# A scan-and-feed-forward kernel: early small reads of the weights, and the masks of two pairs issued in twos

## The chip, the cores and the metric

The kernel runs on one core of one Trainium2 chip. The metric is the device time of one execution in microseconds. Engines are named as in the profile: PE multiplies matrices (PEld loads its weights), DVE is the vector engine, ACT the scalar engine, POOL is GpSimd, SP is the engine that mostly issues DMAs.

## The reference

Two layers follow each other. The first is a chunked state-space scan with 4 batches, 8 heads, 768 positions, 32 channels a head and 16 states; the second is a feed-forward layer with a squared ReLU. Cut to what is computed:

```python
# per batch and head, chunks of 32 positions
cum  = np.cumsum(log_a[chunk]); L = np.exp(cum[i] - cum[j]) * (i >= j)
y    = ((C @ B.T) * L) @ x + (C @ state) * np.exp(cum)
state = np.exp(cum[-1]) * state + sum_j(B[j] x[j] * np.exp(cum[-1] - cum[j]))
# then, over the 3072 tokens, heads side by side (256 features)
h   = np.maximum(y @ w_in, 0.0)      # w_in  256 x 2048
out = h * h @ w_out                  # w_out 2048 x 256
```

The inputs are float32; the two weights are 2 MB each.

## The kernel before

The 3072 tokens are 12 *pairs* (k = 0 to 11), each a batch b and a stretch j of 256 positions; pair k is also block k of the feed-forward layer. A chunk in the kernel is not 32 positions: each pair is treated as two halves of 128 (u = 0, 1), with even and odd positions apart (r = 0, 1). "Third pair" in the change's name is k = 2, "fourth pair" k = 3.

For a pair, the loads of C, B and x come from `ph_load` (line 121; SP issues them), with a hardware queue for SP and another for ACT. The decays come from `a` once for all pairs: `a_nat`, clipped to `a_cl`, scanned to `cp_r`, spread by PE with the matrix `sel` made from the constants `cf` (lines 446, 447, 492 to 530). From there a pair takes these steps:

- `prep_c`, `prep_b`, `prep_x` (lines 145 to 176): scaled copies of C, B and x in bf16, for later pairs on POOL. `prep_x` gives `xs`.
- `ph_tr`, and for k from 4 on a DMA transpose (`ph_dtr`): B and C with states on the partitions, `bct` (line 210).
- `ph_mt` (line 220): PE forms the products of C and B in two PSUM tiles, `mt`, which hold two groups q each.
- `ph_mask` (line 231): DVE multiplies each of the four groups q = 0 to 3 by the causal mask in `cb`, from PSUM to SBUF: `mts`.
- `ph_u` (line 249): PE's update of the state from B and `xs`; `ph_s` (lines 272 to 293) makes the states.
- `ph_y` (lines 307 to 340): the outputs Y from `mts`, `xs` and the states; ACT copies them to `T` (line 359), the feed-forward layer's input.

The feed-forward layer of a block is 8 *steps*, each 256 of the 2048 features: `mm1` (line 370, PE into one of two PSUM slots `hps`), ReLU by ACT to `hb` (line 376), `square` by DVE to `h` (line 382), and `mm2` (line 400) into `ops`. Its weights sit in SBUF as bf16. POOL issues their loads, with a conversion from float32: `load_wi` (line 129) in eight parts of 256 columns of every w_in row, `load_wo` (line 134) in four parts of 512 rows of w_out. They are issued as the work needs them: w_in's first four parts at 4.8 to 9.8 us, w_out's first two from 9.8 us.

The order of all work is written by hand. `steps` lists 96 steps (block, part); for each step s the loop at the end of the kernel issues `mm1`, then what `todo` holds for s (filled by `at`), then the square of step s-1, then an `mm2`, which lags 3 steps, and 4 from step 17 on. So within DVE's queue a mask placed at step s stands ahead of the square of step s-1. Blocks 0 and 1 share the first 16 steps; from step 16 the blocks come one by one. `first_steps` gives the steps of pairs 2 and 3: transposes, U, states, mt, the four masks in a tuple, and Y. Each engine works through its own queue in order, and waits on semaphores. Eight semaphores serve the hardware-queue DMAs in rotation: a DMA waits for the one eight before it.

Of the kernel before, what the change touches and what calls it, by code (L numbers as in the profile page):

```python
# [10 lines left out]
FP32 = mybir.dt.float32  # L11
# [5 lines left out]
def _fap(base: bass.AP, offset_elems: int, free_dims):  # L17

    ap0 = list(base.ap)[0]
    return bass.AP(tensor=base.tensor, offset=base.offset + offset_elems,  # L20
                   ap=[list(ap0)] + [list(d) for d in free_dims])


def _dap(base: bass.AP, offset_elems: int, dims):

    return bass.AP(tensor=base.tensor, offset=base.offset + offset_elems,
                   ap=[list(d) for d in dims])
# [3 lines left out]
def kernel(  # L31
# [14 lines left out]
    nc = tc.nc  # L46
# [5 lines left out]
    const = ctx.enter_context(tc.tile_pool(name="const", bufs=1))  # L52
# [60 lines left out]
    def ph_load(k, order="CBx", eng=None, gate=None):  # L113
        b, j = PAIRS[k]
        t = loaded.setdefault(k, {})
        for what in order:
            src, w = {"B": (B, N), "C": (C, N), "x": (x, D)}[what]
            dst = nat.tile([128, NH, 2 * w], FP32, tag=f"{what}_nat", name=f"{what}_nat{k}")
            if gate is not None:
                gate.memset(dst[:, 0, 0:1], 0.0)  # L120
            (eng or nc.sync).dma_start(
                out=dst, in_=_dap(src, (b * NH * S + j * 256) * w,
                                  [[2 * w, 128], [S * w, NH], [1, 2 * w]]))
            t[what] = dst
# [320 lines left out]
    with tc.manual_schedule():  # L445
        nc.sync.dma_start(out=a_nat, in_=_dap(a, 0, [[256, 96], [1, 256]]))
        nc.scalar.dma_start(out=cf, in_=cf_d.ap())
        ph_load(0, "C")
        ph_load(0, "B")

# [52 lines left out]
        for r in range(2):  # L503
            nc.scalar.copy(out=_fap(C_r, r * 128, [[16, 2], [32, 4], [1, 16]]),
                           in_=_fap(loaded[0]["C"], r * 16, [[128, 2], [32, 4], [1, 16]]))
# [66 lines left out]
        def at(s, fn, *args):  # L572
            todo.setdefault(max(s, 0), []).append((fn, args))
# [18 lines left out]
        for j, s in ((1, 13), (2, 45)):  # L592
            at(s, recip, 0, 4, j)
        first_steps = {
            2: (9, 12, 12, 10, (10, 11, 11, 12), 14),
            3: (17, 21, 21, 18, (18, 19, 19, 20), 22)}
        at(0, ph_mt, 1)
        at(0, warm, 1, 256)
        for i in (1, 0):
# [87 lines left out]
```

## Time and profile before

| | |
|---|---|
| median of 8 runs | 118.78 us |
| lowest and highest | 116.92 and 121.58 us |
| the profiled execution | 117.82 us |
| its span | 116.1 us |
| outside the span | 1.7 us |
| mean DMA rate over the span | 116 GB/s |
| packets under 512 B | 44352 of 50963 |

The profile is of one execution. "Busy" is the time in which an engine works on an instruction; the slices cut the span in 40 parts of 2.9 us. A wait line names the engine and line that waited, after the arrow what released it, then the sum in us, how often, and the longest. A timeline line gives the start, the time from start to end of a group of like instructions, and how many they are; for PE, groups overlap a little since matmuls are pipelined. SPq and ACTq are the issues of DMAs on SP and ACT.

### The profile page before, as it was taken

The numbers are of one execution on the slowest core, as the hardware profiler recorded it, in microseconds if no ns is written. First come the engines' busy times: TensorE is split into PE (matmuls) and PEld (weight loads), VectorE is DVE, ScalarE is ACT, GpSimd is POOL, SyncE is SP. The second block draws the span as 40 slices with busy tenths as digits, with TensorE's granted clock in tenths as the row PEclk, the third lists the DMA queues.
The fourth block names the chain that finished last, engine by engine and source line by source line (L and its number), as shares of the span: only waits on it lengthen the run. The fifth ranks groups of instructions, "written<-read, shape, count | busy, mean of one in ns | idle before, by whom it ended". The sixth has DMA issues, their size and how long they took to land.

```text
span 116.1 us, 4011 instructions
## 1 busy us (share of the span) xinstructions
PE 109.1 (94%) x1639; PEld 88.4 (76%) x1639; DVE 87.0 (75%) x205; ACT 76.1 (66%) x145; POOL 39.0 (34%) x80
## 2 busy tenths in 40 slices
PE   5989879999999999999999999999999999999980
PEld 2545568777787788788887887887887887888970
DVE  6689937599699799798896984994966966935440
ACT  5465957757867577586677586675775865966830
POOL 4669949048594440350414602604300000000000
PEclk9999999999999999999999999999999999999999
DMA  3999999999799812866918628539050020020202
GB/s 71 204 143 151 124 197 180 182 168 177 143 245 228 152 28 90 159 125 126 183 53 162 130 74 160 111 117 217 19 161 3 0 96 0 20 76 0 90 6 90
DMA packets 50963, 13.53 MB, mean 116 GB/s; under 512 B 44352, under 2 KB 50048, under 8 KB 50944
## 3 DMA queue, kind: packets, MB, share of 16 engines
q1 hardware_dynamic: 46400, 10.98, 45.0%
q0 software_dynamic: 4288, 2.10, 14.4%
q8 instruction: 13, 0.21, 0.8%
q10 hardware_dynamic: 256, 0.18, 0.6%
q14 instruction: 6, 0.05, 0.2%
HBM read 10.64 MB, written 3.15 MB: 119 GB/s over the span
## 4 chain that ended last, share of the span: by engine, by line
PE 73%; DMA 14%; DVE 5%; POOL 3%; issue 1%; ACT 0%; SPq 0%; DVEq 0%; POOLq 0%
PE ops L400 31%; PE hps L370 29%; DMA x_nat<-in_x_dram 8%; DMA w_in_b<-in_moe_w_in_dram 4%; PE Y L307 3%; PE mt L220 3%; DMA C_nat<-in_C_dram 2%; DVE mts L231 2%; POOL xs L176 2%; PE Y L336 2%; DVE h L382 1%; PE U L249 1%; PE ctpt L509 1%; PE ops_r L400 1%; DVE bct L526 1%; PE ops L416 1%
## 5 line engine op out<-in xcount | busy, mean ns | idle before, releaser
L376 ACT ACTIVATE hb<-hps 128x512 bf16<-128x512 f32 x96 | 57.5, 599 | 29.7 <-PE hps L370 28.0
L370 PE MATMUL hps<-T,w_in_b 128*128 128x256 bf16 x384 | 57.6, 273 | 0.5 <-DMA w_in_b<-in_moe_w_in_dram 0.3
L400 PE MATMUL ops<-w_out_b,h 128*128 128x256 bf16 x360 | 55.0, 273 | 0.6 <-DMA w_out_b<-in_moe_w_out_dram 0.6
L382 DVE TENSOR_TENSOR h<-hb 128x512 bf16<-128x512 bf16 x96 | 41.6, 457 | 11.1 <-ACT hb L376 11.0
L370 PEld LDWEIGHTS <-w_in_b 128*128 128x128 bf16 x384 | 37.2, 98 | 5.1 <-DMA w_in_b<-in_moe_w_in_dram 0.5
L400 PEld LDWEIGHTS <-h 128*128 128x128 bf16 x376 | 34.5, 98 | 7.0 <-issue 2.6
L231 DVE TENSOR_TENSOR mts<-mt,cb 128x512 bf16<-128x512 f32 x44 | 29.1, 683 | 8.6 <-PE mt L220 8.5
L176 POOL TENSOR_TENSOR xs<-x_nat,Pinv 128x512 bf16<-128x512 f32 x12 | 13.8, 1154 | 10.4 <-DMA x_nat<-in_x_dram 4.0
L145 POOL TENSOR_TENSOR bc<-C_nat,P_sb 128x128 bf16<-128x128 f32 x16 | 6.7, 440 | 24.7 <-DMA C_nat<-in_C_dram 24.7
L293 DVE TENSOR_TENSOR S<-z,Pown 128x256 bf16<-128x256 f32 x16 | 7.9, 496 | 0.5
L485 PE MATMUL dps<-dum 128*128 128x256 bf16 (+1 forms) x25 | 6.3, 366 | 1.3 <-DVE dum L451 1.3
L359 ACT CAST T<-Y 128x512 bf16<-128x512 f32 x11 | 6.4, 586 | 1.1 <-PE Y L340 1.1
L438 ACT COPY osb<-ops 128x512 f32<-128x512 f32 x11 | 6.4, 580 | 0.0
L129 POOL DMA_DIRECT2D w_in_b<-in_moe_w_in_dram x8 | 6.0, 752 | 0.0
L220 PE MATMUL mt<-bct 32*64 32x256 bf16 x192 | 5.1, 280 | 0.3 <-DVE bct L210 0.2
L307 PE MATMUL Y<-mts,xs 64*32 64x128 bf16 x384 | 5.1, 219 | 0.2 <-DVE mts L231 0.2
L170 POOL CAST bc<-B_nat 128x128 bf16<-128x128 f32 x16 | 4.6, 318 | 2.0 <-DMA B_nat<-in_B_dram 1.7
L485 PEld LDWEIGHTS <-dum 128*128 128x128 bf16 x25 | 2.4, 112 | 3.3 <-issue 1.8
L307 PEld LDWEIGHTS <-xs 64*32 64x32 bf16 x384 | 3.1, 91 | 1.9 <-issue 1.0
L220 PEld LDWEIGHTS <-bct 32*64 32x64 bf16 x192 | 1.9, 102 | 2.9 <-issue 1.7
L286 DVE SCALAR_TENSOR_TENSOR z<-z,Ptot,U 128x64 f32<-128x64 f32 x12 | 3.2, 266 | 0.5 <-PE U L249 0.5
L134 POOL DMA_DIRECT2D w_out_b<-in_moe_w_out_dram x4 | 3.1, 792 | 0.3 <-issue 0.3
(77 smaller groups left out, 57.2 us busy)
## 6 DMA issues: line engine op xcount, KB each, us to landing
x_nat<-in_x_dram SPq DMA_DIRECT2D x12, 256.0 KB, 3.7
out_dram<-osb SPq DMA_DIRECT2D x7, 256.0 KB, 2.7
C_nat<-in_C_dram SPq DMA_DIRECT2D x12, 128.0 KB, 2.9
B_nat<-in_B_dram SPq DMA_DIRECT2D x12, 128.0 KB, 3.3
w_in_b<-in_moe_w_in_dram POOLq DMA_DIRECT2D x8, 128.0 KB, 5.6
w_out_b<-in_moe_w_out_dram POOLq DMA_DIRECT2D x4, 256.0 KB, 6.5
out_dram<-osb SPq DMA_DIRECT2D x8, 128.0 KB, 2.3
bct<-bc SPq DMA_TRANSPOSE x8, 3.4
```

The costliest lines, as they stand in the source:

```text
L145: eng.tensor_tensor(out=_fap(bc[k % 3], r * 384 + 128, [[144, 2], [32, 4], [1, 16]]), in0=_fap(loaded[k]["C"], r * 16, [[128, 2], [32, 4], ...
L176: eng.tensor_tensor(out=_fap(xs, 0, [[256, 2], [32, 8], [1, 32]]), in0=_fap(loaded[k]["x"], 0, [[32, 2], [64, 8], [1, 32]]), in1=_fap(Pinv ...
L220: nc.tensor.matmul(mt[q // 2][64 * u:64 * u + 64, q % 2, r, :, :], bct[32 * q:32 * q + 32, r, 0, u * 64:u * 64 + 64], _fap(bct[32 * q:32 * ...
L231: nc.vector.tensor_tensor(out=v["mts"][:, q], in0=v["mt"][q // 2][:, q % 2] if src is None else src, in1=_fap(cb, 128, [[128, 2], [0, 2], ...
L293: nc.vector.tensor_tensor(out=S_n.rearrange("p (g q d) -> p g q d", g=2, q=4), in0=_fap(z, 0, [[32, 2], [0, 4], [1, 32]]), in1=_fap(Pown, ...
L307: nc.tensor.matmul(Y[u][32 * q:32 * q + 32, g, :], v["xs"][64 * u:64 * u + 64, r, h * 32:h * 32 + 32], v["mts"][64 * u:64 * u + 64, q, r, ...
L359: nc.scalar.copy(out=_fap(T[k], 0, [[64, 2], [128, 4], [1, 64]]), in_=_fap(Y[0], 0, [[512, 2], [64, 4], [1, 64]]))
L370: nc.tensor.matmul(hps[:, i, :], w_in_b[:, g, f * 128:(f + 1) * 128], T[blk][:, g].rearrange("p r u t -> p (r u t)"), start=(g == 0), stop ...
L376: nc.scalar.activation(out=hb, in_=hps, func=AF.Relu)
L382: nc.vector.tensor_tensor(out=h2, in0=hb, in1=hb, op=ALU.mult)
L400: nc.tensor.matmul(o[c], h2[:, i, r * 128:(r + 1) * 128], w_out_b[:, f, c * 128:(c + 1) * 128] if len(o) > 1 else w_out_b[:, f, :], start= ...
L485: nc.tensor.matmul(idle[-1][:, 0:cols], dum[:, 0:128], dum[:, 0:cols], start=True, stop=True, skip_group_check=True)
```

## The change

A tile `ahead` is added, which nothing reads. Right after the load of `cf`, ACT issues two more loads: 64 bytes from the start of each of the 256 rows of w_in (8 KB apart), and 64 bytes from every 16 KB of w_out (128 places). In program order they stand after the loads of `a` and `cf`, and before the first loads of C and B.

The masks of pair 2 go from steps (10, 11, 11, 12) to (10, 10, 11, 11), and those of pair 3 from (18, 19, 19, 20) to (18, 18, 19, 19). On DVE the order mask 0, square, masks 1 and 2, square, mask 3, square becomes masks 0 and 1, square, masks 2 and 3, square, square. Nothing else moves on PE, POOL or SP; two more DMAs in the rotation make two of SP's early loads wait for a semaphore.

```diff
         nc.sync.dma_start(out=a_nat, in_=_dap(a, 0, [[256, 96], [1, 256]]))
         nc.scalar.dma_start(out=cf, in_=cf_d.ap())
+
+        ahead = const.tile([128, 3, 16], FP32, name="ahead")
+        nc.scalar.dma_start(out=ahead[:, 0:2, :], in_=_dap(moe_w_in, 0, [[2048, 128], [128 * 2048, 2], [1, 16]]))
+        nc.scalar.dma_start(out=ahead[:, 2, :], in_=_dap(moe_w_out, 0, [[4096, 128], [1, 16]]))
         ph_load(0, "C")
         ph_load(0, "B")
...
         first_steps = {
-            2: (9, 12, 12, 10, (10, 11, 11, 12), 14),
-            3: (17, 21, 21, 18, (18, 19, 19, 20), 22)}
+            2: (9, 12, 12, 10, (10, 10, 11, 11), 14),
+            3: (17, 21, 21, 18, (18, 18, 19, 19), 22)}
```

## The prediction

> **What bounds the kernel now.** I read the page first: engine shares and slices. PE is busy for 94% of the span, at full clock throughout, and its idle tenths stand in the first slices and the last.
>
> ```profile
> PE 109.1 (94%) x1639; PEld 88.4 (76%) x1639; DVE 87.0 (75%) x205; ACT 76.1 (66%) x145; POOL 39.0 (34%) x80
> PE   5989879999999999999999999999999999999980
> DMA  3999999999799812866918628539050020020202
> ```
>
> The rest is therefore read between 0 and 40 us, where the 16 DMA engines are full too. Next the list of PE's waits. Small as they are, they are all that this change can reach:
>
> ```profile
> PE ops L400 <- DMA w_out_b<-in_moe_w_out_dram: 0.6, 1, 0.6
> PE hps L370 <- DMA w_in_b<-in_moe_w_in_dram: 0.3, 1, 0.3
> PE mt L220 <- DVE bct L210: 0.2, 1, 0.2
> PE U L249 <- POOL xs L176: 0.2, 1, 0.2
> PE Y L307 <- DVE mts L231: 0.2, 1, 0.2
> ```
>
> The timeline places them. Columns: start, duration, engine, line, work, count, and idle time before with its releaser.
>
> ```profile
> 13.92 0.61 PE L370 MATMUL hps<-T,w_in_b 128*128 128x256 bf16 x4 [0.33 <-DMA w_in_b<-in_moe_w_in_dram]
> 15.68 0.60 PE L400 MATMUL ops<-w_out_b,h 128*128 128x256 bf16 x4 [0.59 <-DMA w_out_b<-in_moe_w_out_dram]
> ...
> 23.52 1.33 POOL L176 TENSOR_TENSOR xs<-x_nat,Pinv 128x512 bf16<-128x512 f32 x1 [3.08 <-DMA x_nat<-in_x_dram]
> 24.91 0.25 PE L249 MATMUL U<-xs,Bb 64*32 64x64 bf16 x16 [0.20 <-POOL xs L176]
> ...
> 32.38 1.24 DVE L382 TENSOR_TENSOR h<-hb 128x512 bf16<-128x512 bf16 x1
> 33.54 1.27 DVE L231 TENSOR_TENSOR mts<-mt,cb 128x512 bf16<-128x512 f32 x2
> 35.80 0.42 PE L307 MATMUL Y<-mts,xs 64*32 64x128 bf16 x32 [0.20 <-DVE mts L231]
> ```
>
> At 13.92 and 15.68 PE waits for weights. At 24.91 U of pair 2 (the third pair) waits for xs, which waited 3.08 us for its x load, issued at 13.55 and landed 9.80 us later. At 35.80 Y of pair 3 waits for the last mask, with two squares ahead of it on DVE, one of 1.24 us.
>
> [...] a square (both inputs SBUF) takes 0.41 us at the least, but the one of 32.38 took 1.24 while POOL's xs ran from 32.27 to 33.33. A mask has one input in PSUM and takes 0.68 beside the same POOL work. [...]
>
> **The change, part by part.**
>
> *Two issues on ACT.* The one issue seen there (cf) took 0.38 us, so two put the table load from 1.22 to about 2.0. It takes 1.28, the cast 0.30, sel 0.40: sel ends at about 4.0 instead of 3.67, C_r at 4.5 instead of 4.34. PE's first real matmul starts at 4.41 because it needs cp_r's scan as well, and the transposes of C_r start at 5.40. Price 0. Cover: cp_r for sel (0.7 us), PE's own matmuls for C_r (about 0.8). Without it the delay passes on in full.
>
> *384 packets of 64 B.* That is 24 for each DMA engine, between a_nat and C_nat. Lower bound: the packets of 128 B took 13 ns, so 24 x 13 = 0.31 us per engine. Upper bound: cf's packets in the first quarter us of traffic averaged 104 ns, so 2.5 us. The reads are in order and small, as C's are, so I take 0.3. It cannot be below nothing as long as they are read while a_nat and C_nat are queued. a_nat is on the path with no slack (a_cl waited 0.16 us for it), but most of its packets precede: I charge 0.2 us.
>
> *New semaphore waits.* There are eight hardware-DMA semaphores in rotation. With two more DMAs, pair 1's B load now waits for cf and its x load for a_nat. SP reaches these at 3.99 and 4.83; cf and a_nat had landed by 3.27 and 3.52. Behind them on SP stand all later loads. Price 0 while the margins of 0.7 and 1.3 us last.
>
> *What the early touch may remove.* In the trace's packet records most 512 B packets of the weights' queue took 60 ns. Of the first 2048 (the first four w_in loads, two w_out loads, until 16.1 us) 37 took over 150 ns, up to 1378, together 14.9 us over the norm; of the last 2048 nine, 2.1 us. Spread over 16 engines that is 0.93 us each, more on the worst. If these are first accesses, they move to the head. The w_in wait of 0.33 then goes: the next limit is the PSUM slot freed by ACT at 13.57. Y of pair 1 then ends at 14.76 and T at 15.41, against 15.74. The w_out wait of 0.59 shrinks until T is late: the second block's first matmul goes from 16.12 to about 15.45. Both together give 0.67 us, and the T wait is what is late next. x of pair 2 lands behind the same packets; 0.93 us earlier would keep step with PE's 0.67 and take the idle time before U as well: 24.91 less 24.55 (end of the matmuls before), 0.36. Nothing is removed if they are not first accesses. So: 0 to 1.03, taken as 1.03.
>
> *Masks of pair 2.* Each is 0.61 us start to start, a square 0.33. The second mask goes ahead of square 9 and the fourth ahead of square 10, each thus 0.6 later. Square 9 (0.41) would start at 24.13 instead of 23.52, inside xs on POOL: free it costs nothing, as its matmul comes at 25.09. Square 10 would end at 26.06, or at 26.56 if square 9 is held until xs ends; its matmul stood at 25.98. PE loses 0.1 to 0.6; I take 0.4.
>
> *Masks of pair 3.* The last mask has one square less ahead (0.33 us), and the square held at 32.38 now starts at 33.0, so it loses 0.3 instead of 0.8. The idle time before Y (35.80 less 35.45) goes, and so does 0.09 before U at 34.37: 0.44. The limit is then PE's own order. It falls to 0 if square 18 meets xs at 34.90 and keeps its matmul waiting. I take 0.35.
>
> Sum: 0.2 - 1.03 + 0.4 - 0.35 = -0.78 us: the span goes from 116.1 to 115.3, and the profiled execution from 117.82 to 117.0 with the same 1.7 us outside. The median of the eight runs shown is 118.78, 0.96 above it, and they spread over 4.7 us, though the work is the same in each. The DMA waits above are what can vary: if the touch removes what it should, I let it take some six tenths of that gap (an estimate). 118.78 - 0.78 - 0.6 = 117.4.
>
> **The rivals.**
>
> *The touch removes nothing* (chance 0.2). Against the cause assumed: w_in's loads 3 and 4 read the same rows as loads 1 and 2, and had 16 long packets against 5; C, B and x read new memory all the time, and none of their packets took over 60 ns between 2.75 and 30 us. Then 0.2 at the head and 0.3 us of DMA work remain, and the masks cancel: +0.2 to +0.5, 119.1.
>
> *The touch stalls the head: slower* (chance 0.3). One mechanism: the slow first accesses are real but now stand in front of C_nat and B_nat, on the same 16 engines. Price: at 104 ns a packet, 2.5 us. Point from which it decides: Bb by ACT ended at 5.14 and its transpose came at 5.87, so B may land about 0.65 us late; that is 27 ns per packet. At the upper bound 2.5 - 0.65 = 1.85 us pass to pair 0's mt, Y and T. About 0.67 comes back at the weights, and with the squares of pair 2 held (0.6 in place of 0.4) it ends at 118.78 + 1.85 - 0.67 + 0.2 - 0.35 = 119.8 with x unhelped, and up to 121 if the weights come no sooner. I put it at 120.2. Against it: C's and B's own first packets took 13 ns.
>
> **How the numbers follow.** Forecast 0.5, the two rivals 0.2 and 0.3. About 1% (1.2 us) is what a measurement here can tell from no change. The forecast's own range is 116.2 to 118.4, lying past 1% faster with 0.39 and within with 0.11. The second case lies within with 0.16, with 0.03 slower and 0.01 faster. The third lies with 0.27 slower and 0.03 within. Together 0.40, 0.30, 0.30. Range: 116.2 (all waits gone and the whole gap) to 120.3; some 0.07 is left out below and 0.12 above.
>
> **What would show it.** In the profile after: no wait for w_in and w_out at 13.9 and 15.7; x of pair 2 landing in under 9 us; weight packets all near 60 ns; a_cl at 3.7; Y of pair 3 with no mask wait; a new wait of 0.1 to 0.6 for square 10. Wrong if long packets stay where they were, if C_nat lands after 4.5, or if both weight waits remain.

## The result, and the profile after

The changed kernel takes 120.12 us (median of 19 runs, 118.02 to 122.94), the kernel before beside it 118.62 us (52 runs, 116.92 to 121.58): 1.5 us slower. The ratio is 1.0074, with a 95% interval of 1.0039 to 1.011. That ratio leaves out executions over 1.5% above a kernel's fastest, and the change works largely by making long executions frequent, so below I read the medians of all executions, with the span of each. The profiled execution took 121.19 us, its span 119.4.

Engine shares and slices of the changed kernel:

```profile
PE 112.6 (94%) x1639; PEld 89.5 (75%) x1639; DVE 89.6 (75%) x205; ACT 75.9 (64%) x145; POOL 39.0 (33%) x80
PE   5899999998999999999999999999999999999970
DMA  3999999999996912956907818829250020110202
```

PE does the same 1639 matmuls and is busy 3.5 us longer, while the span grew by 3.3. So PE didn't wait more; its matmuls took longer. The list of PE's waits, behind the first (1.3 us ahead of the first warm-up matmul, as before):

```profile
PE ops L400 <- DVE h L382: 0.4, 1, 0.4
PE ctpt L513 <- DVE cp_r L499: 0.3, 1, 0.3
PE mt L220 <- DVE bct L210: 0.2, 1, 0.2
```

Both waits for weights are gone, as forecast, and so is the one for xs. The timeline shows why that is no gain. PE in the head, before:

```profile
4.41 1.19 PE L509 MATMUL ctpt<-cp_r,sel 96*128 96x128 f32 x4 [0.20 <-ACT C_r L504]
...
7.22 0.42 PE L220 MATMUL mt<-bct 32*64 32x256 bf16 x16
7.57 0.83 PE L485 MATMUL dps<-dum 128*128 128x256 bf16 x6
...
10.87 0.60 PE L370 MATMUL hps<-T,w_in_b 128*128 128x256 bf16 x4
```

And after:

```profile
4.52 1.19 PE L513 MATMUL ctpt<-cp_r,sel 96*128 96x128 f32 x4 [0.31 <-DVE cp_r L499]
...
7.64 0.65 PE L220 MATMUL mt<-bct 32*64 32x256 bf16 x16
8.22 1.46 PE L489 MATMUL dps<-dum 128*128 128x256 bf16 x6
...
13.07 0.63 PE L370 MATMUL hps<-T,w_in_b 128*128 128x256 bf16 x4
```

The sixteen mt products took 0.65 us here and 0.42 before, six warm-up matmuls 1.46 and 0.83. These start 0.213 us apart here and 0.109 before: half clock. The clock record of the trace has the full clock granted at 13.12 us of the span, and at 5.47 before. The page's clock row shows nines in both, as the record begins with the first grant. The first mm1 starts at 13.07 instead of 10.87, and by then the weights are there. Y of pair 2 comes at 29.01 instead of 26.95. So 2.2 of the 3.3 us are there by the first mm1. At the last ReLU it is 2.7 us, and 0.5 more are lost behind that, which the part on ACT's issues explains.

ACT and DVE in the head, before:

```profile
1.22 1.28 ACT L490 ACT_TABLE_LOAD   x1 [1.22 <-PEq L671]
...
3.52 0.29 DVE L493 TENSOR_SCALAR a_cl<-a_nat 96x256 f32<-96x256 f32 x1 [0.16 <-DMA a_nat<-in_a_dram]
3.84 0.50 ACT L504 COPY C_r<-C_nat 128x128 f32<-128x128 f32 x2 [0.17 <-DMA C_nat<-in_C_dram]
```

ACT, DVE and POOL after (ACTq is the issue of a DMA):

```profile
1.22 0.56 ACTq L450 DMA_DIRECT2D ahead<-in_moe_w_in_dram  x1
...
1.80 0.57 ACTq L451 DMA_DIRECT2D ahead<-in_moe_w_out_dram  x1
...
2.41 1.28 ACT L494 ACT_TABLE_LOAD   x1 [2.41 <-issue]
...
3.63 0.29 DVE L497 TENSOR_SCALAR a_cl<-a_nat 96x256 f32<-96x256 f32 x1 [0.26 <-DMA a_nat<-in_a_dram]
...
4.66 0.50 ACT L508 COPY C_r<-C_nat 128x128 f32<-128x128 f32 x2 [0.35 <-DMA C_nat<-in_C_dram]
...
4.91 1.62 POOL L129 DMA_DIRECT2D w_in_b<-in_moe_w_in_dram  x2
```

The table load moved from 1.22 to 2.41 us, a_cl from 3.52 to 3.63, C_r from 3.84 to 4.66, the weights' first issue from 4.80 to 4.91. C_r still waits 0.35 us for C's load, although by the packet records the last of C's packets (each load ends with 16 packets of 4 bytes) came at 3.53 us, against 3.46 before.

The squares and masks of pairs 2 and 3:

```profile
28.03 0.61 PE L400 MATMUL ops<-w_out_b,h 128*128 128x256 bf16 x4 [0.39 <-DVE h L382]
...
35.30 1.06 POOL L176 TENSOR_TENSOR xs<-x_nat,Pinv 128x512 bf16<-128x512 f32 x1
...
35.35 1.29 DVE L382 TENSOR_TENSOR h<-hb 128x512 bf16<-128x512 bf16 x1
36.56 1.28 DVE L231 TENSOR_TENSOR mts<-mt,cb 128x512 bf16<-128x512 f32 x2
...
37.89 0.42 PE L307 MATMUL Y<-mts,xs 64*32 64x128 bf16 x32
```

PE's wait of 0.39 for square 10 is the one forecast. At 35.35 a square meets xs and takes 1.29 us, which holds the last masks back: from the start of U of pair 3 (36.43) to that of Y it is 1.46 us, as before (34.37 to 35.80, 1.43).

### The profile page after: what moved, and what is told of

Same layout as the page of the kernel before. It is cut to its first block, busy times and chain, and to the rows that moved or that the text cites. A ratio compares the mean times of both kernels' runs of the same rounds, so it can differ in the third digit from the quotient of the medians.

```text
span 119.4 us, 4013 instructions
## 1 busy us (share of the span) xinstructions
PE 112.6 (94%) x1639; PEld 89.5 (75%) x1639; DVE 89.6 (75%) x205; ACT 75.9 (64%) x145; POOL 39.0 (33%) x80
## 4 chain that ended last, share of the span: by engine, by line
PE 73%; DVE 19%; DMA 2%; issue 1%; ACT 1%; DVEq 0%
PE hps L370 28%; PE ops L400 27%; DVE mts L231 8%; DVE h L382 6%; PE Y L307 4%; PE dps L489 3%; PE mt L220 3%; DVE S L293 3%; DMA a_nat<-in_a_dram 2%; PE Y L336 1%; PE ctpt L513 1%; PE U L249 1%; DVE bct L210 1%; PE Y L340 1%; PE ops_r L400 1%
## 5 line engine op out<-in xcount | busy, mean ns | idle before, releaser
L382 DVE TENSOR_TENSOR h<-hb 128x512 bf16<-128x512 bf16 x96 | 43.3, 476 | 10.6 <-ACT hb L376 10.5
L176 POOL TENSOR_TENSOR xs<-x_nat,Pinv 128x512 bf16<-128x512 f32 x12 | 13.2, 1099 | 9.2 <-DVE z L286 3.7
L293 DVE TENSOR_TENSOR S<-z,Pown 128x256 bf16<-128x256 f32 x16 | 8.9, 557 | 0.5
L489 PE MATMUL dps<-dum 128*128 128x256 bf16 (+1 forms) x25 | 7.9, 449 | 1.3 <-DVE dum L455 1.3
L307 PE MATMUL Y<-mts,xs 64*32 64x128 bf16 x384 | 5.7, 226 | 0.3
L489 PEld LDWEIGHTS <-dum 128*128 128x128 bf16 x25 | 3.0, 136 | 3.9 <-issue 2.2
L170 POOL CAST bc<-B_nat 128x128 bf16<-128x128 f32 x16 | 5.3, 361 | 1.0 <-DMA B_nat<-in_B_dram 1.0
```

What stands on the lines that cost most here:

```text
L176: eng.tensor_tensor(out=_fap(xs, 0, [[256, 2], [32, 8], [1, 32]]), in0=_fap(loaded[k]["x"], 0, [[32, 2], [64, 8], [1, 32]]), in1=_fap(Pinv ...
L293: nc.vector.tensor_tensor(out=S_n.rearrange("p (g q d) -> p g q d", g=2, q=4), in0=_fap(z, 0, [[32, 2], [0, 4], [1, 32]]), in1=_fap(Pown, ...
L307: nc.tensor.matmul(Y[u][32 * q:32 * q + 32, g, :], v["xs"][64 * u:64 * u + 64, r, h * 32:h * 32 + 32], v["mts"][64 * u:64 * u + 64, q, r, ...
L382: nc.vector.tensor_tensor(out=h2, in0=hb, in1=hb, op=ALU.mult)
L489: nc.tensor.matmul(idle[-1][:, 0:cols], dum[:, 0:128], dum[:, 0:cols], start=True, stop=True, skip_group_check=True)
```

## The experiments

Each kernel computes the whole reference, and each ran beside the kernel before on its chip. "Difference" is median minus the median of before there; its 95% interval comes from resampling the executions of both. "Long" counts spans of 118.3 us or more; of before's executions beside the experiments 28 of 287 are long. Of these 28, 19 have a mean granted clock of 0.991 or less; of the 24 long ones of the change and of the early loads alone, only 2. So what the change makes frequent is not what makes most of before's long ones.

| kernel | executions | median, us | difference | median span | long |
|---|---|---|---|---|---|
| the change (spans: the profiled one too) | 19 | 120.12 | +1.50 (0.80 to 2.02) | 118.4 | 12 of 20 |
| early loads alone | 22 | 120.41 | +1.80 (1.06 to 2.28) | 118.5 | 12 of 22 |
| masks alone | 22 | 118.93 | +0.32 (-0.30 to 0.71) | 117.2 | 3 of 22 |
| two loads of 16 rows | 6 | 120.12 | +1.51 (1.04 to 2.14) | 117.8 | 2 of 6 |
| early loads from SP | 22 | 119.74 | +1.13 (0.46 to 1.60) | 118.0 | 6 of 22 |
| unused tile of 192 bytes | 6 | 119.78 | +1.43 (0.49 to 2.28) | 117.9 | 2 of 6 |
| early loads, 512-byte tile | 6 | 119.22 | +0.87 (0.48 to 2.26) | 117.4 | 1 of 6 |
| the change, 512-byte tile | 24 | 119.26 | +0.91 (0.45 to 1.49) | 117.5 | 6 of 24 |
| masks of pair 3 alone | 22 | 118.82 | +0.48 (-0.16 to 0.70) | 116.5 | 2 of 22 |
| the change, gap filled | 22 | 119.60 | +1.17 (0.42 to 1.54) | 117.9 | 6 of 22 |
| before, gap filled | 22 | 118.47 | +0.03 (-0.46 to 0.32) | 116.7 | 1 of 22 |
| before, gap widened | 22 | 118.66 | +0.23 (-0.39 to 0.70) | 116.8 | 3 of 22 |
| before, two gaps filled | 22 | 118.47 | +0.04 (-0.53 to 0.41) | 116.8 | 1 of 22 |
| unused tile of 64 bytes | 22 | 119.45 | +0.68 (0.10 to 1.36) | 117.6 | 3 of 22 |
| unused tile of 512 bytes | 22 | 118.73 | -0.05 (-0.49 to 0.72) | 116.8 | 4 of 22 |
| early loads from SP, 512-byte tile | 22 | 118.91 | +0.14 (-0.51 to 0.73) | 117.1 | 0 of 22 |
| a_nat aligned too | 14 | 118.37 | -0.41 (-0.75 to -0.01) | 116.5 | 1 of 14 |
| only C, B, x shifted | 23 | 119.29 | +0.82 (0.24 to 2.12) | 117.3 | 8 of 23 |
| only the weights shifted | 22 | 118.88 | +0.41 (-0.20 to 1.09) | 117.0 | 4 of 22 |

**Which part costs.** The early loads with the old masks:

```diff
+        ahead = const.tile([128, 3, 16], FP32, name="ahead")
+        nc.scalar.dma_start(out=ahead[:, 0:2, :], in_=_dap(moe_w_in, 0, [[2048, 128], [128 * 2048, 2], [1, 16]]))
+        nc.scalar.dma_start(out=ahead[:, 2, :], in_=_dap(moe_w_out, 0, [[4096, 128], [1, 16]]))
```

> The early loads alone, masks where they were. Head theory (the loss of the whole change is made before the first matmul of the feed-forward layer, by the late ACT queue and the late landing of a and C, and it is multiplied because TensorE's full clock is then granted later in more of the executions): all or nearly all of the loss is here, median 119.6 to 120.2 us against 118.6 for the kernel before. Mask theory (the loss is the wait of square 10's matmul, 0.39 us in the profile after): this one is level with the kernel before, within 0.3 us. First-touch theory: weights land sooner and this one is faster, 117.8 or less.

The masks alone:

```diff
-            2: (9, 12, 12, 10, (10, 11, 11, 12), 14),
-            3: (17, 21, 21, 18, (18, 19, 19, 20), 22)}
+            2: (9, 12, 12, 10, (10, 10, 11, 11), 14),
+            3: (17, 21, 21, 18, (18, 18, 19, 19), 22)}
```

> The masks alone, no early loads. Mask theory: 0.4 to 0.9 us slower than before (119.0 to 119.5), with a wait of 0.4 us or more before the matmul of square 10 of the order. Head theory: within 0.3 us of before, the 0.4 lost at the third pair partly given back at the fourth.

Two loads issued by ACT in the same places, with 32 packets in place of 384:

```diff
+        nc.scalar.dma_start(out=ahead[0:16, 0, :], in_=_dap(moe_w_in, 0, [[2048, 16], [1, 16]]))
+        nc.scalar.dma_start(out=ahead[0:16, 2, :], in_=_dap(moe_w_out, 0, [[4096, 16], [1, 16]]))
```

> Masks as before; the two early loads shrunk to 16 rows each (32 packets instead of 384, so next to nothing is fetched early), issued at the same place on ACT. If the loss comes from the two issues ahead of ACT's table load: as slow as the full early loads (119.6 to 120.2), table load at about 2.2 to 2.4 us. If it comes from the packets ahead of a, C and B: level with before, 118.6 within 0.3, and a_cl back at 3.52 us. Leaves out most of the early bytes; nothing reads them.

The 384 packets issued by SP behind the first x load, so that ACT is untouched:

```diff
         ph_load(0, "x")
+        ahead = const.tile([128, 3, 16], FP32, name="ahead")
+        nc.sync.dma_start(out=ahead[:, 0:2, :], in_=_dap(moe_w_in, 0, [[2048, 128], [128 * 2048, 2], [1, 16]]))
+        nc.sync.dma_start(out=ahead[:, 2, :], in_=_dap(moe_w_out, 0, [[4096, 128], [1, 16]]))
```

> Masks as before; the same 384 early packets, issued by SP after the first x load, so neither ACT nor a, C and B of the first pair stand behind them, and they are still read before the first weight load. Head theory: level with before, 118.6 within 0.3 us. First-touch theory: the benefit without its price, 117.8 or less, with weight packets near 60 ns and no PE wait for weights. If the packets themselves hurt wherever they stand: slower by 0.3 us or more.

The early loads carry the loss (+1.80), and the masks' +0.32 can't be told from nothing. But 32 packets lose as much as 384 (in six executions), and the loads still lose 1.13 us where ACT's table load stays at 1.22 us. So neither the packets nor ACT's delay can be the whole. The packet records say the same: the 384 packets of 64 B took 11 ns each and 38 at most, none was long, and the weights' long packets stayed. In the first 2048 weight packets 38 took over 150 ns (37 before), in the last 2048 there were 33 (9 before). Over all traces the first 2048 have 26 to 53 such packets without early loads and 35 to 46 with all 384 of them, so the early reads take none away.

All four kernels with a loss share two things. They issue two DMAs more, to which the part on ACT's issues comes back. And the tile `ahead` of 192 bytes per partition stands ahead of C_r, the weights and C, B and x in SBUF. Before, C_nat, B_nat, x_nat, w_in_b and w_out_b all start at multiples of 512 bytes; with the tile they start 192 bytes past one.

**The place alone.** An unused tile of that size in that spot, and nothing loaded:

```diff
+        pad = const.tile([128, 3, 16], FP32, name="pad")
```

> The kernel before with an unused tile of 192 bytes per partition where the change puts its early tile: every later tile stands at the address it has in the changed kernel, nothing more is loaded, and the masks are as before. Placement theory (the loss comes from tiles of the head that no longer start at a multiple of 512 bytes, so that their loads are seen later and PE's full clock comes late more often): 119.6 to 120.5 us median, as with the early loads alone (120.41); C_r starts at 4.3 to 4.8 us of the span. Loads theory (the early loads themselves cost): level with before, 118.3 to 118.9 us, and C_r at 3.8 to 4.0.

The early loads with their tile made 512 bytes, `[128, 8, 16]`, and then the whole change with such a tile:

> The early loads alone, with their tile padded from 192 to 512 bytes per partition, so that the later tiles start at multiples of 512 bytes again; masks as before. Placement theory: level with before within 0.4 us (118.3 to 119.0 us), C_r at 3.9 to 4.1 us. Loads theory: no better than the early loads alone, 119.9 to 120.6 us, C_r at 4.6 to 4.8.

> The whole change with the tile of the early loads padded to 512 bytes. Placement theory: only the masks' 0.3 us remain, 118.6 to 119.2 us. Loads theory: as the changed kernel, 119.8 to 120.5 us.

The unused tile gives 119.78 us (ratio 1.0126, 1.0061 to 1.0191), in six executions only. The larger tile brings the whole change from +1.50 to +0.91 and early loads on ACT to +0.87: between the two theories. Later runs looked at the placement alone, with unused tiles of 64 and of 512 bytes, `[128, 1, 16]` and `[128, 8, 16]`:

> The kernel before with an unused tile of 64 bytes per partition, so that C_nat, B_nat, x_nat, w_in_b and w_out_b start 64 bytes past a multiple of 512; nothing is loaded early. Placement theory (loads whose destinations do not start at a multiple of 512 bytes are seen later by the engines in the head): 119.3 to 120.3 us, a_cl at 3.6 to 3.75 us, C_r at 4.3 to 4.8. Rival (only the early transfers cost): 118.2 to 118.8 us, a_cl at 3.3 to 3.5, C_r at 3.8 to 4.1.

> The kernel before with an unused tile of 512 bytes per partition: everything is shifted, but the later tiles start at multiples of 512 bytes again. Placement theory: level with before, 118.2 to 118.8 us, a_cl at 3.3 to 3.5 us. Rival (any shift costs): 119.3 to 120.3 us.

512 bytes shift as many tiles and cost nothing (-0.05); 64 bytes cost 0.68. That speaks for where the tiles start, and against the shift as such. The times alone don't settle it: the two differ by 0.73 us with an interval of -0.11 to 1.46, and the ratio for 64 bytes, 0.9972 (0.9909 to 1.0034), shows no loss. The traces below show the effect itself. Which tiles? An unused tile behind the weights, or one ahead of them with another of 320 bytes behind:

```diff
     w_out_b = wpool.tile([128, 16, 256], BF16, name="w_out_b")
+    pad1 = wpool.tile([128, 48], FP32, name="pad1")
```

> The kernel before with an unused tile of 192 bytes behind the weights' tiles: C_nat, B_nat, x_nat and all that lies behind start 192 bytes past a multiple of 512, the weights and C_r stay where they are. If the head's loads of C and B are what the shift hurts: 119.2 to 120.0 us, C_r at 4.3 to 4.8 us and a_cl at 3.5 to 3.75. If it is the weights: 118.3 to 118.9 us, C_r at 3.8 to 4.1.

> The kernel before with an unused tile of 192 bytes ahead of C_r and the weights and one of 320 bytes behind them: w_in_b, w_out_b and C_r start 192 bytes past a multiple of 512, C_nat, B_nat, x_nat and all behind at multiples of 512. If the head's loads of C and B are what the shift hurts: 118.3 to 118.9 us, C_r at 3.8 to 4.1. If it is the weights: 119.2 to 120.0 us.

Only C, B, x and what lies behind shifted: +0.82 (ratio 1.0034, 1.0003 to 1.0066). Only the weights and C_r: +0.41, not told from nothing, nor from the other by its time. The head shows the difference in single lines of the timelines. Kernel with an unused tile of 512 bytes:

```profile
3.29 0.29 DVE L494 TENSOR_SCALAR a_cl<-a_nat 96x256 f32<-96x256 f32 x1
...
3.82 0.50 ACT L505 COPY C_r<-C_nat 128x128 f32<-128x128 f32 x2 [0.31 <-DMA C_nat<-in_C_dram]
```

Kernel with only C, B and x shifted:

```profile
3.77 0.29 DVE L494 TENSOR_SCALAR a_cl<-a_nat 96x256 f32<-96x256 f32 x1 [0.41 <-DMA a_nat<-in_a_dram]
...
4.33 0.50 ACT L505 COPY C_r<-C_nat 128x128 f32<-128x128 f32 x2 [0.49 <-DMA C_nat<-in_C_dram]
```

C's last packet comes at 3.47 us in both, but C_r starts 0.51 later. The 16 signals that C's load sends to its semaphore come from 3.50 to 3.80 us in the first and from 3.94 to 4.31 in the second. Over all traces C_r starts at 3.78 to 4.13 us in the ten kernels whose C_nat starts at a multiple of 512 and whose ACT issues nothing more, and at 4.29 to 4.77 in the eight where it doesn't. a_cl starts at 3.49 to 3.77 in those eight and at 3.29 to 3.59 in the ten, though a_nat moved in one kernel only (the one with a_nat aligned, a_cl at 3.36). For B the engines notice no delay: its cast Bb starts at 4.84 to 5.36 us in those ten, and at 5.04 to 5.28 in the four of the eight where ACT issues nothing more.

The difference doesn't end with the head. The queue of SP's DMAs on the two pages (packets, MB, share of 16 engines), with the unused tile of 512 bytes (span 120.4 us) and with C, B and x shifted (119.6):

```profile
q1 hardware_dynamic: 46400, 10.98, 43.9%
...
q1 hardware_dynamic: 46400, 10.98, 47.8%
```

The same bytes keep each DMA engine busy for 52.9 and 57.2 us. Over all traces it is 51.8 to 53.1 us in the twelve kernels whose C, B and x start at multiples of 512, and 54.7 to 57.4 in the eight others. C's packets take 13 ns in all of them, but the 256-byte packets of the first x load 17.8 to 17.9 ns in the twelve and 18.7 to 23.6 in the eight. That the start of these tiles slows DMAs is thus shown. How much of the time lost is due to C, B and x and how much to tiles behind them, which moved as well (the outputs' `osb` among them), is not.

**ACT's issues.** The early loads from SP with a 512-byte tile, against the same from ACT (+0.87, and +0.91 with the masks):

> The early loads issued by SP behind the first x load (ACT untouched), with their tile padded to 512 bytes; masks as before. If placement and the two issues on ACT are the whole loss: 118.2 to 118.8 us. If the early transfers and their issue cost in themselves: 119.0 to 119.6 us, as with the padded tile and the issues on ACT (119.22 and 119.26 us).

+0.14 in the medians (-0.51 to 0.73) lies between the two forecasts, and the ratio, 1.0041 (1.0008 to 1.0075), speaks for half a us. With the tiles in place and ACT left alone, the early loads bring nothing and still cost something.

The traces show what, at the very end of the kernel. The two DMAs turn the rotation of the semaphores, so that the last three stores signal numbers 109, 99 and 101 instead of 107, 108 and 109. SP ends the kernel by waiting for the semaphores one after another in rising order, some 0.06 us for each. Before, the last store to land has the last number, and SP's waits are over 0.04 us after it. With the early loads seven waits are left then, and they take 0.41 us. It is so in all eight kernels that issue the two DMAs, by ACT or SP, with 32 packets or 384, whatever the tile, and in none of the twelve others: 0.37 us, in every trace.

What the issues cost on ACT is less sure. On ACT and from SP the early loads with the 512-byte tile differ by 0.73 us (0.05 to 2.12, the former in six executions), but the ratio for the whole change with that tile is 1.0021 (0.9985 to 1.0057). The kernel with the 512-byte tile and the loads on ACT shows the delay there:

```profile
2.42 1.28 ACT L494 ACT_TABLE_LOAD   x1 [2.42 <-issue]
...
4.39 0.50 ACT L508 COPY C_r<-C_nat 128x128 f32<-128x128 f32 x2
```

C_r starts as late as with a shifted C, right behind sel (3.91 us, 0.40 long). C's last signal came at 4.37 here; in the whole change with such a tile it came at 4.14, and C_r still started only at 4.21. ACT itself comes late.

**How a later head becomes 1 to 3 us.** In the traces the stretch at full clock lasted a multiple of 3.413 us (112.64 us before, 33 of them; 105.81 us after, 31), and the grants fall at 4.0 to 6.4, 10.1 to 10.7, or 12.4 to 13.1 us. Leaving out three traces in which the clock fell back and one that lost time later on (1.06 us for a mask, and 1.8 at its end, where the last store landed late), spans are 116.1 to 117.9 us with the first, 116.8 to 116.9 with the second (where later waits for weights seem to hide part of it), and 119.0 and 119.4 with the third, which two traces have. Of executions that were not traced the grant is not known, so that late grants make most of the changed kernel's long ones is likely, not shown. The early loads alone, profiled with a grant at 4.11 us:

```profile
6.89 0.42 PE L220 MATMUL mt<-bct 32*64 32x256 bf16 x16 [0.30 <-DVE bct L530]
7.24 0.83 PE L489 MATMUL dps<-dum 128*128 128x256 bf16 x6
...
10.54 0.60 PE L370 MATMUL hps<-T,w_in_b 128*128 128x256 bf16 x4
```

Its span is 116.5, 0.4 above before's, about what the waits at the end add: in this execution, with its early grant, the rest of the loss is gone. What decides when the grant comes the traces don't show; that the idle gap between the first warm-up and ctpt does was my assumption. I tested it by filling or widening that gap with warm-up matmuls of 0.21 us:

```diff
         warm(6)
-        warm(1, 256)
+        warm(3, 256)
```

> The changed kernel with two more 128x256 matmuls at the end of the first warm-up, 0.21 us each at half clock, so that PE has no gap between 4.21 us and its first real matmul (0.31 us in the changed kernel). Clock theory (the loss is PE's full clock coming at 12 to 13 us instead of 4 to 6 us in more executions[...]): 118.2 to 119.0 us median, full clock before 7 us. Rival (the loss has nothing to do with this gap: later loads alone): 119.8 to 120.6 us.

The same with `warm(2, 256)` on the kernel before, without that line on the kernel before, and with one more `warm(1, 256)` ahead of btr:

> The kernel before with one more 128x256 matmul at the end of the first warm-up: its gap of 0.20 us ahead of ctpt is closed. Clock theory: 117.8 to 118.3 us median, 0.2 to 0.6 us faster than before, with fewer long executions. Rival: level with before or slower by up to 0.2 us (the added matmul delays ctpt where cp_r is early).

> The kernel before with one 128x256 matmul fewer in the first warm-up: the gap ahead of ctpt grows from 0.20 to 0.41 us, the gap of the kernels with the early loads (0.31 to 0.41 us); loads, tiles and masks are untouched. Clock theory: 119.3 to 120.5 us median, the loss of the change without any of its parts. Rival: level with before within 0.3 us, since no real work starts later.

> As the kernel before with its first gap closed, and one more 128x256 matmul ahead of btr's transposes, where PE waits 0.43 us for the cast of B. Clock theory: 117.6 to 118.3 us, no slower than with the first gap closed alone. Rival: 118.4 to 118.9 us.

In the changed kernel filling the gap halves the long executions (12 of 20 to 6 of 22) but takes only 0.3 us off the difference, well within its interval; its profiled execution has the grant at 4.43 us and, with a wait of 1.32 us for w_in, a span of 117.9. The kernel before gains nothing from it and loses nothing measurable from a shorter warm-up (in its profile cp_r came early, and the gap was 0.24 us instead of 0.41). The clock theory's forecasts for these four all failed in the medians. So this gap is a part at most; what else in the later head makes the grant late stays open.

**Masks of pair 3, and a try at a better kernel.** The kernel before with only pair 3 in twos, and the kernel before with a_nat at a multiple of 512 as well (480 unused bytes ahead of it, 32 behind):

> The kernel before with only the fourth pair's masks in twos; the third pair's stand as before. If the masks' 0.3 us come from the third pair (mm2 of step 10 waits 0.4 to 0.5 us for its square): 118.2 to 118.6 us, that is 0 to 0.4 us faster than before, and no wait of mm2 for a square. If the fourth pair's order costs as well: 118.8 to 119.1 us.

> The kernel before with two unused tiles (480 bytes before a_nat, 32 bytes behind) so that a_nat too starts at a multiple of 512 bytes; all later tiles as with the pad of 512 bytes. If the start of a load's own destination decides when it is seen: a_cl at 3.2 to 3.3 us (it is held at 3.27 by DVE's own work) in place of 3.3 to 3.5, and 118.0 to 118.4 us. If not: level with before, 118.3 to 118.8 us.

The masks of pair 3 take away Y's wait in that profile (U waits 0.2 us for a mask instead), but the time is no better (+0.48, within its interval of nothing; ratio 1.0053, 1.0024 to 1.0083). Aligning a_nat gives 118.37 us, 0.41 below before in its round, but its ratio is 0.9975 with 0.9938 to 1.0011: a hint, not a gain that I would claim. No kernel tried is shown to beat the kernel before.

## Why the prediction was wrong

The forecast was 117.4 us and faster; it is 120.12 and slower. The value lies inside the range of 116.2 to 120.3, on the side of the second rival (120.2), but by another mechanism.

- *"What the early touch may remove", -1.03.* This step failed. The touch removed nothing: the long packets stayed (37 and 38 in the first 2048), and the early packets took 11 ns, so no access there was slow by being first. The waits for weights at 13.9 and 15.7 us are gone from the profile after, where PE came late for them; with an early grant they are back (0.33 and 0.53 us with the early loads alone), and they are also gone in the profile of the masks alone, which loads nothing early. The estimated 0.6 us of the gap between median and profile fell with it. The first rival had this right.
- *A term that was missing: the tile.* The tile for the early bytes moved the destinations of C, B and x off multiples of 512 bytes. I followed the instructions that the change adds, and not the memory they take. Cost by itself: 0.68 us (64 bytes), 0.82 (C, B and x alone), 1.43 (192 bytes, six executions), of a loss of 1.50. With the other terms this comes to more than 1.50; the intervals are too wide for a sum.
- *Another: PE "at full clock throughout".* The page's clock row begins with the first grant. Before's full clock came at 5.47 us, so it could come later, and no term priced that. In the profile after it came at 13.12, and 2.2 of the 3.3 us lost there stand by the first mm1.
- *"Two issues on ACT", "Price 0".* The issues took 0.56 and 0.57 us, not 0.38, so the table load came at 2.41 instead of "about 2.0", sel ended at 4.31 instead of 4.0, and C_r, held by a late C as well, ended at 5.16 instead of 4.5. The cover that I named ended; the difference of 0.73 us between early loads on ACT and from SP is its rough price.
- *"384 packets of 64 B", 0.2 us on a_nat.* The packets cost 0.26 us per engine (24 of 11 ns), near the lower bound. a_cl came 0.11 later, which the placement can explain: the unused tile of 192 bytes alone has a_cl at 3.65.
- *"New semaphore waits", 0.* For the two waits at the start that holds nearly: SP's issue of pair 1's B took 1.18 us instead of 0.80, its x load was issued at 5.10 instead of 4.83, and no cost of it was seen. But the rotation was followed at the start only. At the end it leaves six waits more behind the last store, 0.37 us.
- *"Masks of pair 2", +0.4.* Right: PE waits 0.39 us for square 10, and 0.5 with the masks alone.
- *"Masks of pair 3", -0.35, and 0 "if square 18 meets xs".* That case came: the square of 35.35 took 1.29 us beside xs (35.30 to 36.36) and ended 0.28 us behind it, where 81 of this profile's 96 squares took 0.43 us at most. With the masks alone, where xs ran earlier, Y waits for no mask.
- *The second rival* had the sign and nearly the time, but its mechanism, slow early packets in front of C and B, did not occur: 11 ns a packet, under its own deciding point of 27, and C's last packet only 0.07 us later. Its chain, from a late C to pair 0's mt, Y and T, did.
- *What would show it.* "Long packets stay where they were" and "C_nat lands after 4.5" (C_r waited for it until 4.66) both came true, as named among the signs that the forecast is wrong.

## What to carry to other kernels

A new tile, even one that nothing reads, moves every tile behind it: compare the addresses of DMA destinations before and after a change, and pad a small tile to the step that they keep (an unused tile of 64 bytes gave +0.68 us here, one of 512 bytes -0.05). Where DMAs take semaphores in rotation, follow a new DMA to the last store: it can leave waits behind it (0.37 us here). Price a "free" instruction on a start-up engine by the chain behind it, here table load, sel, C_r. Where a short kernel's executions spread by more than the effect, compare the spans of all executions and look where PE gets its full clock (at 5.47 us before, at 13.12 after); one profile can show either case.

## What the runs showed of the hardware

- Where C, B and x start 64 or 192 bytes past a multiple of 512 in SBUF, the first C is seen by ACT about 0.5 us later, though its packets (13 ns each) end at the same time; the 256-byte packets of the first x load take 18.7 to 23.6 ns instead of 17.8 to 17.9, and SP's queue keeps the DMA engines busy for 54.7 to 57.4 us instead of 51.8 to 53.1. What makes the difference is not shown, and no run here has a shift of 128 or 256 bytes.
- The full clock can also be lost again. In three traces PE waited 1.4 to 1.7 us for w_out near 15 us, and then ran at half clock for 3.41 us (mean granted clock 0.979 to 0.981, in all other traces 0.996 or more); the spans were 119.9 to 120.4 (the last with 1.8 us at its end, where the last store landed late). In two others waits of 1.36 and 1.72 us had no such effect. In the kernel with the early loads and the 512-byte tile (PE's timeline; a group of four takes 0.60 at full clock):

```profile
16.46 0.89 PE L400 MATMUL ops<-w_out_b,h 128*128 128x256 bf16 x4 [1.71 <-DMA w_out_b<-in_moe_w_out_dram]
17.14 1.06 PE L370 MATMUL hps<-T,w_in_b 128*128 128x256 bf16 x4
```

- SP's closing waits for semaphores take some 0.06 us each. Seven behind the last landing took 0.41 us, one 0.04.
- Issuing a DMA from ACT took 0.50 to 0.59 us for the early loads, 0.38 for cf.
